# Two attention layers with 32 heads of 16, blended by a gate: products with V in wider pieces, and a new order of steps over four rounds

## The chip, the cores and the metric

The kernel runs on one core of one Trainium2 chip. The metric is the device time of one execution in microseconds. "Before" is the kernel as it stood, "after" the one with the change.

## The reference

Two attention layers A and B read the same `x` (2048 tokens of 512) with weights of their own, and a gate blends their outputs:

```python
def layer(x, wqkv, wo):                      # B, S, D = 1, 2048, 512;  H = 32, Dh = 16
    qkv = (x @ wqkv).reshape(B, S, 3, H, Dh).transpose(2, 0, 3, 1, 4)
    q, k, v = qkv[0], qkv[1], qkv[2]
    scores = jnp.einsum("bhqd,bhkd->bhqk", q, k) * (Dh ** -0.5)
    p = _softmax(scores, axis=-1)
    o = jnp.einsum("bhqk,bhkd->bhqd", p, v)
    return o.transpose(0, 2, 1, 3).reshape(B, S, D) @ wo

g = _sigmoid((x * gate_w).sum(-1, keepdims=True))
return g * layer(x, A_wqkv, A_wo) + (1 - g) * layer(x, B_wqkv, B_wo)
```

All inputs and the output are float32.

## The kernel before

Two layers of 32 heads make 64 heads, and every head has 16 tiles of 128 tokens, so there are 64 * 16 = 1024 **rounds** (`ROUNDS`). A prologue (up to about 288 us) projects q, k and v, keeps q and k as sums of two float16 parts in DRAM (`qd`, `kd`) and v in DRAM (`vd`). After that the loop `while r < ROUNDS` does the attention, and the output projection of finished layers is fed in between.

A head's q and k lie stacked on partitions in `q_st[h % 3]` and `k_st[h % 3]`, once in the lower and once in the upper 64 partitions (`load_stacks` fills both by 12 DMAs of SP's queue). One **bank** is a PSUM tile of 128 x 512, filled by four matmuls that each use a tile of 64 rows x 32 columns of TensorE's array. There are two sets of four such tiles: `tiles_of(0)` and `tiles_of(1)`. Products with V always use set 0, and `next_tiles` gives a bank of scores to the set that has had less to do, counted in `load`.

The work of the loop is of five kinds, and a letter stands for each in the string `FULL`:

- `e`: one bank of scores of keys against queries (`score`, L220), on which ScalarE then computes the exponential into the tile `p` in SBUF (L222). The bank is one of four named `ps_st`.
- `m`: one bank of scores of queries against keys of a head that comes later (`max_plain`), of which VectorE takes the maximum of each row (L158). The bank is one of three named `ps_m`.
- `D`: a bank of `ps_st` whose positive part ScalarE writes to SBUF as `rise` (`max_rise`, L165); `A`: a bank of `ps_m` to which VectorE adds that `rise` and takes the maximum of the sum (`max_pair`, L170). Each such pair replaces two banks of maxima.
- a digit: so many blocks of 128 queries of the product of `p` with V (`attend_next`, `attend`, L720), added up over 16 tiles of keys in the one bank `acc`. A digit is cut where a tile `p` ends after four blocks, and what is left is one **piece**: one instruction group of four matmuls over 128, 256, 384 or 512 columns. After each 16 tiles `p`, VectorE or ScalarE copies `acc` to SBUF (`attended`, L743), and SP's queue writes it to DRAM.
- `Q` and `R`: one step of the queue `row_ops` (small work of VectorE and ScalarE), if there is one. At the end of a head's maxima, the queue gets `max_split`, three empty steps and `max_rows`: the latter transposes the row maxima on VectorE (L187), writes them to DRAM (L190) and reads them back as two further rows of `q_st` (L192), which the head's `e` banks need.

`FULL` holds one **pass** over four rounds: 16 `e`, 12 `m`, 2 `D`, 2 `A`, and 32 blocks of products with V. It is run for r = 2, 6, ..., 998, so 250 times; the last 22 rounds use the string `LATE` instead. The string is the order in which the instructions are issued: each engine works through its own instructions in this order and waits at semaphores for the others. Products with V lag behind the exponentials by four tiles `p` (eight `e`), of the eight buffers that there are.

```python
            elif step.isdigit():
                for a in projects:
                    project_out(*a)
                    load[:] = [0, 0]
                projects.clear()
                for _ in range(attend_next(int(step))):
```

Steps of the output projection come due at given rounds (`due`). Their loads, sums and splits run on SP's queue and GpSimd; `project_out` itself (L587, 12 or 9 matmuls over the whole array, then VectorE) goes ahead of the first digit, four tiles of 128 tokens at a time.

Of the kernel before, what the change touches and what calls it, by code (L numbers as in the profile page):

```python
# [54 lines left out]
def gated_mha(ctx: ExitStack, tc: tile.TileContext, xT, x, wqkv_a, wo_a, wqkv_b, wo_b, gate_w, out):  # L55
# [703 lines left out]
                ended += u % 2  # L759
        return ended  # L760

    FULL = "QDQemQ2e1m1e2em1Qe1m2eQ1Dm1e2AQ1em1e3mem1e1Q2e1m1e1m1e1m1e1RQ2mReA"
    LATE = "e2" * 8
    projects, row_ops = [], []

# [15 lines left out]
    while r < ROUNDS:  # L781
        m = r + NT + LEAD
        if m >= ROUNDS and not ring:
            ring.append(6)
        order = FULL if m < ROUNDS else LATE
        n = order.count("e") // 4
# [70 lines left out]
```

## Time and profile before

| | |
|---|---|
| median of 3 runs | 2845.35 us (2840.07 to 2850.31) |
| profiled execution | 2855.93 us, span of the trace 2854.1 us |
| mean granted clock of TensorE | 0.994 |
| TensorE matmul busy (PE) | 2589.7 us, 91% |
| TensorE weight load busy (PEld) | 1856.0 us, 65% |
| VectorE busy (DVE) | 2405.9 us, 84% |
| ScalarE busy (ACT) | 2414.3 us, 85% |
| GpSimd busy (POOL) | 325.3 us, 11% |
| first and last `D` of a pass on ScalarE | 287.7 and 2773.8 us |

The busy time of matmuls is a union of overlapping intervals whose ends are modelled, since matmuls are pipelined and two sets of tiles work side by side; it is no measure of how full the array is. In the trace a float32 matmul and its weight load each stand as two instructions, so a piece of four matmuls makes 8 matmuls and 8 weight loads, and a bank of scores (float16) makes 4 and 4. A row of the timeline or of the groups names line, engine, operation, what is written and read, and the shape; "x" is the count; what stands behind a bar or in brackets is the idle time of the engine just before, and what ended it. "issue" there is idle time of the engine that no wait for another engine explains.

### The profile page before, as it was taken

The page shows a single profiled execution, that of the slowest core. Times are in us where ns is not written, and L with a number is a line of the kernel's source. Part 1 is how long each engine was busy: PE and PEld are TensorE (multiplying, and loading weights), DVE is VectorE, ACT ScalarE, POOL GpSimd, SP SyncE. Part 2 cuts the span into 40 slices and gives each one's busy share as a digit, 9 for nine tenths or more (in the row PEclk, how much of TensorE's full clock was granted, in tenths as well). Part 3 has the DMA queues.
Part 4 walks back from the last instruction along what each step waited for, and adds up shares of the span by engine and source line. Part 5 has one row for each costly group of instructions (what it writes and reads, how often), then busy time and mean ns, then how long its engine had stood idle before and what let it go on. Part 6 is the DMA issues. An engine that isn't in the chain of part 4 may idle for free.

```text
span 2854.1 us, 181748 instructions
## 1 busy us (share of the span) xinstructions
PE 2589.7 (91%) x83094; PEld 1856.0 (65%) x83094; DVE 2405.9 (84%) x4538; ACT 2414.3 (85%) x4794; POOL 325.3 (11%) x583
## 2 busy tenths in 40 slices
PE   9999898999999988898888898999989988888898
PEld 7787666666666666666666666666666666666664
DVE  4434898999999999999888777899999999988784
ACT  4222999999999999999999776899999999988696
POOL 2010211110000000000100432000000001022303
PEclk9999999999999999999999999999999999999999
DMA  5352222211111111111112232111111121123112
GB/s 201 113 164 97 64 58 69 60 51 41 54 39 47 46 56 45 47 46 52 52 44 73 87 106 65 40 48 45 56 37 44 46 60 56 45 66 103 61 32 106
DMA packets 110938, 187.09 MB, mean 66 GB/s; under 512 B 27944, under 2 KB 46744, under 8 KB 110168
## 3 DMA queue, kind: packets, MB, share of 16 engines
q1 hardware_dynamic: 106456, 164.97, 18.1%
q8 instruction: 650, 10.65, 1.6%
q0 software_dynamic: 2560, 8.91, 1.1%
q10 hardware_dynamic: 1152, 1.57, 0.2%
q14 instruction: 120, 0.98, 0.1%
HBM read 109.33 MB, written 66.05 MB: 61 GB/s over the span
## 4 chain that ended last, share of the span: by engine, by line
PE 68%; DVE 14%; issue 9%; ACT 5%; DMA 3%; SPq 1%; POOL 0%; ACTq 0%; DVEq 0%; POOLq 0%
PE acc L720 30%; PE ps_st L220 13%; PE ps_m L152 12%; DVE mxp L158 10%; PE ps_st L300 6%; ACT p L222 4%; PE ps_st L353 3%; PE ps_m L587 3%; DVE rise L170 2%; PE ps_st L152 2%; DMA o_part<-od 1%; DVE ev L743 1%; ACT ev L743 1%; ACT rise L165 1%; DMA q_st<-qd 0%
## 5 line engine op out<-in xcount | busy, mean ns | idle before, releaser
L222 ACT ACTIVATE p<-ps_st 128x512 f32<-128x512 f32 x4051 | 2146.5, 675 | 208.7 <-PE ps_m L152 104.5
L720 PE MATMUL acc<-p,vg 64*17 64x128 f32 (+2 forms) x48672 | 2066.3, 308 | 157.7 <-issue 139.9
L158 DVE TENSOR_REDUCE mxp<-ps_m 128x1 f32<-128x512 f32 x3048 | 1920.8, 682 | 208.0 <-PE ps_m L152 130.6
L220 PE MATMUL ps_st<-q_st,k_st 50*32 50x512 f16 x16220 | 1640.6, 381 | 46.8 <-issue 36.0
L720 PEld LDWEIGHTS acc<-p,vg 64*17 64x17 f32 x48672 | 1325.1, 93 | 385.0 <-issue 238.0
L152 PE MATMUL ps_m<-k_st,q_st 48*32 48x512 f16 x14192 | 1486.4, 381 | 42.7 <-issue 30.2
L152 PEld LDWEIGHTS <-q_st 48*32 48x32 f16 x16384 | 584.1, 90 | 317.0 <-issue 212.3
L220 PEld LDWEIGHTS <-k_st 50*32 50x32 f16 x16384 | 582.7, 90 | 205.9 <-issue 129.5
L170 DVE CUSTOM_DVE_ANT_0 rise<-ps_m,rise 128x512 f32<-128x512 f32 x500 | 341.6, 683 | 29.9 <-PE ps_m L152 14.3
L165 ACT ACTIVATE rise<-ps_st 128x512 f32<-128x512 f32 x500 | 337.0, 674 | 5.6 <-PE ps_st L152 4.8
L152 PE MATMUL ps_st<-x_st,q_st 48*32 48x512 f16 x2000 | 210.6, 380 | 4.0 <-issue 2.7
L180 POOL TENSOR_SCALAR mrow<-mrow 128x16 f32<-128x16 f32 x64 | 16.5, 257 | 1724.9 <-DVE mrow L179 1724.9
L320 ACT ACTIVATE parts<-ps_st 128x512 f16<-128x512 f32 x64 | 38.0, 596 | 112.2 <-PE ps_st L300 105.5
L321 DVE SCALAR_TENSOR_TENSOR parts<-ps_st,parts 128x512 f16<-128x512 f32 x64 | 44.0, 691 | 96.2 <-ACT parts L320 90.1
L356 ACT COPY v_st<-ps_st 128x512 f32<-128x512 f32 x32 | 18.8, 588 | 82.1 <-PE ps_st L353 80.2
L587 PE MATMUL ps_m<-wo,ot 128*128 128x512 f32 x348 | 84.5, 398 | 2.1 <-DVE mxp L158 1.9
L587 PEld LDWEIGHTS ps_m<-wo,ot 128*128 128x128 f32 x348 | 65.6, 191 | 19.7 <-issue 3.5
L559 POOL TENSOR_TENSOR o_num<-o_num,o_part 128x512 f32<-128x512 f32 x32 | 40.8, 1276 | 234.2 <-DMA o_part<-od 234.2
L300 PE MATMUL ps_st<-xh,whi 128*128 128x512 f32 x224 | 59.9, 389 | 0.0
L300 PE MATMUL ps_st<-xh,wlo 128*128 128x512 f32 x224 | 59.9, 389 | 0.0
L300 PE MATMUL ps_st<-xl,whi 128*128 128x512 f32 x224 | 59.9, 389 | 0.0
L300 PEld LDWEIGHTS ps_st<-xh,wlo 128*128 128x128 f32 x224 | 42.0, 188 | 8.7
(122 smaller groups left out, 994.7 us busy)
## 6 DMA issues: line engine op xcount, KB each, us to landing
od<-ev SPq DMA_DIRECT2D x126, 256.0 KB
k_st<-kd SPq DMA_DIRECT2D x128, 128.0 KB
q_st<-qd SPq DMA_DIRECT2D x128, 128.0 KB
vd<-v_st SPq DMA_DIRECT2D x32, 272.0 KB
vg<-vd POOLq DMA_DIRECT2D x32, 272.0 KB, 3.5
qd<-parts SPq DMA_DIRECT2D x32, 256.0 KB
kd<-parts SPq DMA_DIRECT2D x32, 256.0 KB
k_st<-kd SPq DMA_DIRECT2D x128, 64.0 KB
```

The costliest lines, as they stand in the source:

```text
L152: pe.matmul(ps[j:j + 32], q[b:b + SC, t * P + j:t * P + j + 32], k[b:b + SC], start=True, stop=True, tile_position=(b, j))
L158: dve.tensor_reduce(o[:, c:c + 1], ps, op=ALU.max, axis=AX.X)
L165: act.activation(rises[m], ps, AF.Relu)
L170: dve.tensor_tensor_reduce(out=rise, in0=ps, in1=rise, scale=1.0, scalar=LOWEST, op0=ALU.add, op1=ALU.max, accum_out=o[:, 0:1])
L220: pe.matmul(ps[j:j + 32], k[b:b + SC + 2, kk * P + j:kk * P + j + 32], q[b:b + SC + 2, cc * 512:(cc + 1) * 512], start=True, stop=True, ti ...
L222: act.activation(pt[u][:, c * 512:(c + 1) * 512], ps, AF.Exp, scale=SCALE / UNIT ** 2)
L300: pe.matmul(ps, w[a][:, k], (xh, xl)[b][cc][:, k], start=n == 0, stop=n == 3 * KC - 1)
L321: dve.scalar_tensor_tensor(pt[1][:, sl], ps, UNIT, pt[0][:, sl], op0=ALU.mult, op1=ALU.subtract)
L353: pe.matmul(ps, a[:, k, o:o + P], b[:, k], start=n == 0, stop=n == 3 * KC - 1)
L587: pe.matmul(ps, ot[a][:, slot, tt * P:(tt + 1) * P], wt[b][:, g], start=first and i == 0, stop=last and i == 2)
L720: pe.matmul(acc[d:d + 17, qa * P:qb * P], v[b:b + 64, 2 * (w % n) + c if h == NH - 1 else w % n, j], pt[u][b:b + 64, c * 512 + qa * P:c * ...
L743: (dve.tensor_copy if w < NT or h == NH - 2 else act.copy)(ev, acc)
```

## The change

One line differs: the string `FULL`. It holds the same 16 `e`, 12 `m`, 2 `D`, 2 `A`, 8 `Q`, 2 `R` and 32 blocks in another order, and the blocks stand in 12 digits (2 2 4 3 1 4 4 3 1 2 2 4) where there were 24 (mostly 1 and 2, one 3). No digit of either string is cut further.

```diff
-    FULL = "QDQemQ2e1m1e2em1Qe1m2eQ1Dm1e2AQ1em1e3mem1e1Q2e1m1e1m1e1m1e1RQ2mReA"
+    FULL = "QQD2mee2me4mQemQe3Dme1m4eme4Qme3eARRQe1m2eme2me4QeQmeA"
```

TensorE, in the first pass, before: a piece of one block between a bank of `m` and a bank of `e` (each bank is four such pairs of weight load and matmul, of which the one next to the piece is shown; `x4` are the four tiles of the array).

```order
L152 LDWEIGHTS q_st_165
L152 MATMUL ps_m<-k_st_166,q_st_165 32x512
L720 MATMUL acc<-raw,vg 17x128 x4
L220 LDWEIGHTS k_st_161
L220 MATMUL ps_st<-q_st_160,k_st_161 32x512
```

And after, in a later pass, at the first `4` of the string:

```order
L220 LDWEIGHTS k_st_161
L220 MATMUL ps_st<-q_st_160,k_st_161 32x512
L720 MATMUL acc<-p,vg 17x512 x4
L220 LDWEIGHTS k_st_161
L220 MATMUL ps_st<-q_st_160,k_st_161 32x512
```

One piece of 512 columns stands where four blocks were issued in several pieces with banks between them. On TensorE the program has 72354 such rows before and 69354 after; the 3000 that are gone are 12 pieces of each of 250 passes.

VectorE, around the end of a head's maxima, before: the copy of `acc`, the last maxima of the head (L158, L170), `max_split` (L179) and `max_rows` (L187).

```order
L158 TENSOR_REDUCE mxp<-ps_m 128x1 x6
L743 COPY ev<-acc 128x512
L158 TENSOR_REDUCE mxp<-ps_m 128x1
L170 ISA rise,mxp<-ps_m,rise 128x512
L170 ISA mxp 128x1
L179 TENSOR_REDUCE mrow<-mxp 128x16
L158 TENSOR_REDUCE mxp<-ps_m 128x1 x4
L187 STREAM_TRANSPOSE mt<-mparts 128x32
L158 TENSOR_REDUCE mxp<-ps_m 128x1
```

And after:

```order
L158 TENSOR_REDUCE mxp<-ps_m 128x1 x3
L743 COPY ev<-acc 128x512
L158 TENSOR_REDUCE mxp<-ps_m 128x1
L170 ISA rise,mxp<-ps_m,rise 128x512
L170 ISA mxp 128x1
L179 TENSOR_REDUCE mrow<-mxp 128x16
L158 TENSOR_REDUCE mxp<-ps_m 128x1 x7
L187 STREAM_TRANSPOSE mt<-mparts 128x32
L158 TENSOR_REDUCE mxp<-ps_m 128x1
```

The copy of `acc` stands ahead of the same one `m` and the `A`; the transposition of the row maxima has moved from behind four `m` to behind seven. In the string it stood behind the sixth `e` of a pass, and now stands behind the eighth. The instructions of GpSimd and of SP's queue stand in the same order as before.

## The prediction

> **What bounds the kernel now.** I read the page first, for the shares of the engines and the queues.
>
> ```profile
> span 2854.1 us, 181748 instructions
> PE 2589.7 (91%) x83094; PEld 1856.0 (65%) x83094; DVE 2405.9 (84%) x4538; ACT 2414.3 (85%) x4794; POOL 325.3 (11%) x583
> ...
> q8 instruction: 650, 10.65, 1.6%
> ...
> PE 68%; DVE 14%; issue 9%; ACT 5%; DMA 3%; SPq 1%; POOL 0%; ACTq 0%; DVEq 0%; POOLq 0%
> ```
>
> Three engines are nearly full, and 9% of the chain that ended last is "issue": TensorE waits, and no other engine is the reason. Queue q8 carries instructions: 10.65 MB in 650 packets is 16384 bytes each. TensorE has 83094 + 83094 = 166188 recorded instructions; over 650 packets that is 255.7 each. So I take q8 for TensorE's own instructions, 256 a packet, 64 bytes each.
>
> Next, the waits in a stretch of the loop without output projection (600 to 1400 us): who waited for what, us in total, times, longest.
>
> ```profile
> PEld acc L720 <- issue: 79.4, 116, 1.5
> PEld L152 <- issue: 77.3, 224, 1.6
> ...
> PE acc L720 <- issue: 42.6, 87, 1.2
> PEld L220 <- issue: 34.5, 84, 1.2
> DVE mxp L158 <- PE ps_m L152: 33.5, 84, 1.1
> ACT p L222 <- PE ps_st L220: 22.2, 56, 1.1
> ...
> PEld acc L720 <- ACT ev L743: 6.9, 14, 0.9
> PEld acc L720 <- DVE ev L743: 6.7, 14, 0.8
> ```
>
> VectorE and ScalarE wait for TensorE, and TensorE for "issue". Where do those waits end? I took them from the timeline and asked for the time from one end to the next (length; busy and count by engine):
>
> ```profile
> 903.27 0.27 PE L720 MATMUL acc<-p,vg 64*17 64x128 f32 x1 [0.58 <-issue]
> ...
> 884.18:888.20 4.02, 3.04 (x128) 2.40 (x128) 3.82 (x8) 3.64 (x8) 0.00 (x0) 1.00 0.06 12
> 888.20:891.94 3.74, 3.29 (x128) 2.38 (x128) 3.25 (x7) 3.01 (x7) 0.00 (x0) 1.00 0.02 4
> 903.27:906.73 3.46, 3.04 (x128) 2.57 (x128) 2.91 (x7) 3.46 (x8) 0.00 (x0) 1.00 0.28 97
> 906.73:910.75 4.02, 3.31 (x128) 2.38 (x128) 3.79 (x8) 3.81 (x9) 0.91 (x2) 1.00 0.09 23
> ```
>
> From one stall to the next TensorE runs 128 matmuls and 128 weight loads, exactly 256, in all four rows, whatever these are. That is one packet of q8: TensorE has run dry of instructions, and a refill takes 3.46 to 4.02 us. The stretch as a whole says the same.
>
> ```profile
> 600.00:1400.00 800.00, 721.01 (x26921) 516.48 (x26908) 746.86 (x1428) 770.75 (x1538) 36.76 (x117) 1.00 0.17 48
> ...
> q8 instruction: 210, 3.44, 1.9%
> ```
>
> 210 refills in 800 us are 3.81 us each, inside the range that the stalls give: the stream of instructions runs at its own limit nearly all the time. The Trainium skill (Runtime: NRT & Kernel Launch, section "Instruction fetch mechanics") has refills in blocks of 16 KiB, 256 instructions, with which these rows agree; it also says that fetch is hidden, since dispatch is slower than refill, and gives TensorE room for 2048 instructions. The stalls after every 256 speak against that part here.
>
> **The passes.** Two `D` stand in each pass, so the count of L165 gives passes per stretch (length; busy and count on ScalarE):
>
> ```profile
> 290.00:600.00 310.00, 43.43 (x64) 1.00 0.21 62
> 600.00:1400.00 800.00, 111.86 (x169) 1.00 0.17 48
> 1400.00:1570.00 170.00, 21.34 (x34) 1.00 0.18 53
> 1570.00:1800.00 230.00, 24.10 (x36) 0.97 0.25 80
> 1800.00:2540.00 740.00, 106.50 (x156) 1.00 0.17 49
> 2540.00:2775.00 235.00, 29.12 (x41) 0.96 0.22 67
> ```
>
> The four ordinary stretches hold 423 `D`, 211.5 passes, in 2020 us: 9.55 us a pass. The two with output projection hold 38.5 passes in 465 us: 12.08 us. A pass of before has 32 banks of scores with 8 instructions each and 24 pieces with 16 (4 float32 matmuls and 4 weight loads, each in two): 256 + 384 = 640, or 2.5 refills; at 3.81 us that is 9.53 us. The 9.55 are explained.
>
> **What the change removes.** 12 pieces of 16 instructions in each of 250 passes: 192 of 640 go. 448 are left, 1.75 refills, at 3.81 us 6.7 us a pass. The stream is then no longer the limit, and what is late next has to be found: the two engines that empty the banks, or the array.
>
> Their pace without a wait, from rows in which they work back to back (start, length, count):
>
> ```profile
> 927.37 3.04 ACT L222 ACTIVATE p<-ps_st 128x512 f32<-128x512 f32 x6
> 930.24 0.67 ACT L165 ACTIVATE rise<-ps_st 128x512 f32<-128x512 f32 x1
> ...
> 931.69 4.27 DVE L158 TENSOR_REDUCE mxp<-ps_m 128x1 f32<-128x512 f32 x7
> 935.88 0.68 DVE L170 CUSTOM_DVE_ANT_0 rise<-ps_m,rise 128x512 f32<-128x512 f32 x1
> 936.48 0.08 DVE L170 DVE_READ_ACCUMULATOR2_ANT mxp<- 128x1 f32 x1
> 936.48 0.68 DVE L158 TENSOR_REDUCE mxp<-ps_m 128x1 f32<-128x512 f32 x1
> ```
>
> ScalarE: (930.24 - 927.37) / 6 = 0.478 us a bank. A pass has 16 `e` and 2 `D`, and a copy of `acc` every fourth pass, taken at the same pace: 18.25 x 0.478 = 8.72 us. VectorE: (935.88 - 931.69) / 7 = 0.599 us an `m`, 0.60 an `A`: 14 x 0.60 = 8.39, a copy of `acc` every fourth pass (0.15), and a head's small steps, some 0.1: 8.65 us. So a pass can't go below 8.72 us, and both engines are within 0.1 us of that.
>
> The array: a piece costs what its columns cost. Instances of L720 by shape:
>
> ```profile
> L720 PE MATMUL acc<-p,vg 64*17 64x128 f32 x11440 | 473.9, 270 | 35.8 <-issue 35.5
> L720 PE MATMUL acc<-p,vg 64*17 64x256 f32 x4036 | 347.3, 378 | 11.0 <-issue 7.1 <-ACT ev L743 1.6 <-DVE ev L743 0.4
> L720 PE MATMUL acc<-p,vg 64*17 64x384 f32 x676 | 76.0, 483 | 0.0
> ...
> 903.53 0.54 PE L720 MATMUL acc<-p,vg 64*17 64x384 f32 x4
> 903.72 0.39 PE L220 MATMUL ps_st<-q_st,k_st 50*32 50x512 f16 x4
> 903.86 0.54 PE L720 MATMUL acc<-p,vg 64*17 64x384 f32 x4
> 903.94 0.39 PE L152 MATMUL ps_m<-k_st,q_st 48*32 48x512 f16 x4
> ```
>
> Each further 128 columns add 105 to 108 ns, so a block costs 2 x 0.107 = 0.21 us in whatever piece (a piece is issued in two halves). 32 blocks are 6.8 us of set 0, in both orders. The banks of scores run beside them: one starts at 903.72 between the two halves of the 384-column piece, the next at 903.94, 0.22 us later. 32 x 0.22 = 7.0 us on set 1. Both are under 8.72, so the array covers what goes and does not replace it.
>
> **What is moved.** Wider pieces bunch the array's work, and the 3 + 4 banks between TensorE and the other two must cover the bunches. The longest is `m4eme4Qm`: a 512-column piece should hold set 0 for 4 x 0.21 = 0.86 us, in which set 1 can fill four banks; nothing starves if scores overtake as above. No row shows 512 columns; bounds: 0 if they behave as the 384 do, and at the far end what the third rival prices. I take 0.05 us a pass for this.
>
> The piece reads a `p` whose last `e` lies at least five `e` back (six before). There are four `ps_st` banks, so the fifth `e` could be issued only after that bank had been emptied: the wait costs nothing. The copy of `acc` is followed by five banks until the next piece where there were six; the waits for it are 6.9 + 6.7 us in 84 passes now, 0.16 a pass, and I allow 0.08 more.
>
> `max_rows` moves from behind the sixth `e` to behind the eighth, and SP's rows show its slack:
>
> ```profile
> 883.86 0.58 SPq L190 DMA_DIRECT2D md<-mt  x1
> 885.83 0.55 SPq L192 DMA_DIRECT2D q_st<-md  x2
> 893.77 0.56 SPq L114 DMA_DIRECT2D k_st<-kd  x1
> ```
>
> The write takes 1.97 us until its data may be read back; if the read takes as long after its issue at 886.1, it has landed at 888.4. The reload of the old head's stack goes out at 893.77, when its last scores are done and those of the new head begin: 5.4 us of slack. Two `e` of 0.6 us and a pass that is 0.7 us shorter take 1.9 of it. 3.5 are left: nothing. The loads and stores of SP and GpSimd keep their order and rounds, and come 7% sooner with slack of rounds.
>
> **The sum.** A pass of 8.72 + 0.05 + 0.08 = 8.85 us in the ordinary stretches: 211.5 x (9.55 - 8.85) = 148 us. In the two stretches with projection, `project_out` keeps all three engines waiting in bursts that don't change; I take half the gain for their passes: 38.5 x 0.35 = 13 us. Together 161 us. The profiled execution took 2855.93 us and would take 2695; the median of the runs is 10.6 us under it, 2845.35 - 161 = 2684. I say 2685.
>
> **Rivals.** First, the bunches cost more than I allow. Only 7 banks cover them, and VectorE and ScalarE must both be kept 98% busy from one queue of instructions; before, ScalarE reached 770.75 of 800 us, or 96%, in finer steps. At 95% of ScalarE's floor a pass takes 9.18: 250 x 0.37 = 92, or 2753 us; down to no gain at 9.5.
>
> Second, the "issue" waits aren't the limit, or don't shrink with the count: TensorE would lose as much per pass with 448 instructions, in fewer and longer waits, and the time stays at 2845 +- 8.5 (0.3%, about what a measurement can tell from no change). The 256 between stalls speak against it. By the Trainium skill's statement that fetch is hidden (same page and section) the gain would be 0, the time 2845, and the 9% of "issue" something else.
>
> Third, slower: a 512-column piece doesn't let scores pass. If the four of a pass ran alone, TensorE would need 4 x 0.86 + 7.0 = 10.4 us, and more with the two pieces of 384. That is 0.9 us over before, 250 x 0.9 = 225: 3070 us. It becomes a loss where the two sets lose over 9.55 - 7.0 = 2.55 us a pass of their side by side. The 384-column row speaks against it.
>
> **Numbers.** Forecast 0.67 (2640 to 2730), bunches 0.20 (2730 to 2835), no change 0.06, slower 0.07. The low end of the range is a pass at its floor everywhere: 250 x 0.83 = 207, 2638, so 2640. The upper end takes in most of the first rival: 2765. Faster 0.87, same 0.06, slower 0.07.
>
> **What would show it.** q8 with 462 packets ((166188 - 48000) / 256); no stall of "issue" each 256 instructions, and its share of the chain at 2% or less; ScalarE at 97% or more between 600 and 1300 us; L165 counted 2 per 8.85 us; 512-column matmuls at about 590 ns (483 + 107), with scores starting inside them. I am wrong if TensorE's waits for `ps_m` or `ps_st` leave ScalarE under 95%, if refills take much longer than 4 us, or if the piece behind the copy of `acc` waits over 0.5 us a pass.

## The result, and the profile after

| | before | after |
|---|---|---|
| median of 4 runs | 2843.68 us (2840.07 to 2850.31) | 2689.16 us (2687.98 to 2691.21) |
| span of the profiled execution | 2854.1 us | 2686.2 us |
| a pass in the ordinary stretches | 9.55 us | 8.99 us |
| a pass in the stretches with output projection | 12.08 us | 10.99 us |

The ratio is 0.9455, with a 95% interval from 0.9436 to 0.9474. The forecast was 2685 us.

The page of after, the lines that answer to those shown of before:

```profile
span 2686.2 us, 133748 instructions
PE 2591.5 (96%) x59094; PEld 1441.2 (54%) x59094; DVE 2388.0 (89%) x4538; ACT 2374.2 (88%) x4794; POOL 325.1 (12%) x583
...
q8 instruction: 462, 7.57, 1.2%
...
PE 53%; ACT 24%; DVE 14%; issue 7%; DMA 2%; SPq 0%; POOL 0%; ACTq 0%; DVEq 0%; POOLq 0%
```

TensorE has 48000 instructions fewer and q8 has 462 packets, both as forecast. ScalarE's part of the chain that ended last has risen from 5% to 24%. The waits of after between 600 and 1300 us, the longest first, without those of GpSimd:

```profile
PEld L152 <- issue: 108.9, 405, 0.5
PEld L220 <- issue: 105.4, 519, 0.7
...
PEld acc L720 <- ACT ev L743: 17.2, 20, 0.9
...
PEld acc L720 <- DVE ev L743: 13.9, 19, 0.9
...
DVE mxp L158 <- PE ps_st L220: 4.7, 16, 0.3
```

"PE acc L720 <- issue", 42.6 us before in a slightly longer stretch, is no longer in the list, nor are ScalarE's and VectorE's waits of 22 and 33 us for TensorE. What is left under "issue" are weight loads that stand idle 0.2 to 0.3 us at a time while matmuls run.

The same stretch by engine (length; busy and count):

```profile
600.00:1300.00 700.00, 676.01 (x17478) 350.60 (x17462) 685.59 (x1322) 698.83 (x1426) 26.02 (x93) 1.00 0.17 50
```

And the count of `D` on ScalarE by stretch of after:

```profile
290.00:1480.00 1190.00, 242.49 (x265) 1.00 0.18 54
1480.00:1698.00 218.00, 33.92 (x38) 0.99 0.29 93
1698.00:2400.00 702.00, 141.44 (x156) 1.00 0.17 52
2400.00:2605.00 205.00, 34.55 (x39) 1.00 0.21 69
```

ScalarE is busy 698.83 of 700 us: it is the limit now, at 700 / 1426 = 0.491 us an operation. VectorE follows with 685.59. 421 `D` in 1892 us are 8.99 us a pass, and 77 in 423 us are 10.99.

### The profile page after: what moved, and what is told of

Read it like the earlier page. It is cut to its first block, busy times and chain, and to the rows that moved or that the text cites. A ratio compares the mean times of both kernels' runs of the same rounds, so it can differ in the third digit from the quotient of the medians.

```text
span 2686.2 us, 133748 instructions
## 1 busy us (share of the span) xinstructions
PE 2591.5 (96%) x59094; PEld 1441.2 (54%) x59094; DVE 2388.0 (89%) x4538; ACT 2374.2 (88%) x4794; POOL 325.1 (12%) x583
## 4 chain that ended last, share of the span: by engine, by line
PE 53%; ACT 24%; DVE 14%; issue 7%; DMA 2%; SPq 0%; POOL 0%; ACTq 0%; DVEq 0%; POOLq 0%
ACT p L222 20%; PE acc L720 18%; PE ps_m L152 11%; PE ps_st L220 10%; DVE mxp L158 10%; PE ps_st L300 6%; PE ps_st L353 3%; DVE rise L170 3%; PE ps_m L587 3%; ACT ev L743 2%; ACT rise L165 2%; DMA o_part<-od 1%; PE ps_st L152 1%; DVE mrow L179 0%; DVE ev L743 0%
## 5 line engine op out<-in xcount | busy, mean ns | idle before, releaser
L222 ACT ACTIVATE p<-ps_st 128x512 f32<-128x512 f32 x4051 | 2200.8, 861 | 87.7 <-PE ps_st L220 83.7
L720 PE MATMUL acc<-p,vg 64*17 64x256 f32 (+3 forms) x24720 | 2005.0, 448 | 64.1 <-ACT ev L743 33.8
L158 DVE TENSOR_REDUCE mxp<-ps_m 128x1 f32<-128x512 f32 x3048 | 1895.1, 681 | 76.4 <-PE ps_st L152 43.5
L220 PE MATMUL ps_st<-q_st,k_st 50*32 50x512 f16 x16220 | 1554.9, 381 | 6.3 <-issue 0.3
L152 PE MATMUL ps_m<-k_st,q_st 48*32 48x512 f16 x14192 | 1409.0, 379 | 14.6 <-DVE mxp L158 3.2
L220 PEld LDWEIGHTS <-k_st 50*32 50x32 f16 x16384 | 649.5, 90 | 501.9 <-issue 342.3
L152 PEld LDWEIGHTS <-q_st 48*32 48x32 f16 x16384 | 596.0, 90 | 476.1 <-issue 353.3
L720 PEld LDWEIGHTS acc<-p,vg 64*17 64x17 f32 x24720 | 544.5, 92 | 179.4 <-issue 56.8
L165 ACT ACTIVATE rise<-ps_st 128x512 f32<-128x512 f32 x500 | 454.7, 909 | 0.0
L170 DVE CUSTOM_DVE_ANT_0 rise<-ps_m,rise 128x512 f32<-128x512 f32 x500 | 341.6, 683 | 18.1 <-PE ps_st L220 2.0
L743 ACT COPY ev<-acc 128x512 f32<-128x512 f32 x62 | 53.7, 866 | 0.0
```

The costliest lines, as they stand in the source:

```text
L152: pe.matmul(ps[j:j + 32], q[b:b + SC, t * P + j:t * P + j + 32], k[b:b + SC], start=True, stop=True, tile_position=(b, j))
L158: dve.tensor_reduce(o[:, c:c + 1], ps, op=ALU.max, axis=AX.X)
L165: act.activation(rises[m], ps, AF.Relu)
L170: dve.tensor_tensor_reduce(out=rise, in0=ps, in1=rise, scale=1.0, scalar=LOWEST, op0=ALU.add, op1=ALU.max, accum_out=o[:, 0:1])
L220: pe.matmul(ps[j:j + 32], k[b:b + SC + 2, kk * P + j:kk * P + j + 32], q[b:b + SC + 2, cc * 512:(cc + 1) * 512], start=True, stop=True, ti ...
L222: act.activation(pt[u][:, c * 512:(c + 1) * 512], ps, AF.Exp, scale=SCALE / UNIT ** 2)
```

## The experiments

Each kernel was timed beside the kernel before. "Ordinary" and "projection" are the lengths of a pass in the two kinds of stretches, taken between the same `A` steps in each trace (9.60 and 12.06 us for before, 8.99 and 10.99 for after, on this count). Before took 2843.68 us beside after, 2849.92 beside e1 to e4, 2851.92 beside e5 to e8 and 2831.26 beside e9 to e12. Differences to after are those of the times; by the ratios they would be some 6 to 9 us smaller for e6 and e8 and 9 to 14 us larger for e9 to e12. The lengths of the passes, which need no second kernel, agree with the times to some 3 us.

| run | instructions a pass | time, us | ordinary | projection |
|---|---|---|---|---|
| before | 640 | 2843.68 | 9.60 | 12.06 |
| after | 448 | 2689.16 | 8.99 | 10.99 |
| e1, new order, 24 pieces | 640 | 2854.16 | 9.56 | 11.85 |
| e2, new order, 18 pieces | 544 | 2705.33 | 8.99 | 11.38 |
| e3, new order, 32 pieces | 768 | 3281.96 | 11.39 | 13.52 |
| e4, old order, 12 pieces | 448 | 2709.70 | 8.97 | 11.72 |
| e5, scores in halves | 704 | 3070.67 | 10.49 | 12.79 |
| e6, after, more on ScalarE | 448 | 2829.69 | 9.57 | 11.43 |
| e7, before, more on ScalarE | 640 | 2889.67 | 9.72 | 12.28 |
| e8, new order, 8 pieces | 384 | 2721.54 | 9.11 | 11.16 |
| e9, after, rows earlier | 448 | 2715.02 | 8.99 | 11.71 |
| e10, after, rows later | 448 | 2687.75 | 8.98 | 10.93 |
| e11, old order, 12 pieces, rows later | 448 | 2685.44 | 8.96 | 11.13 |
| e12, after, split on VectorE | 448 | 2744.00 | 9.18 | 11.46 |

The first four separate the number of pieces from the order of the steps.

```diff
 after: FULL = "QQD2mee2me4mQemQe3Dme1m4eme4Qme3eARRQe1m2eme2me4QeQmeA"
 e1:    FULL = "QQD11mee11me22mQemQe21Dme1m112eme22Qme21eARRQe1m11eme11me112QeQmeA"
 e2:    FULL = "QQD11mee2me22mQemQe3Dme1m22eme22Qme3eARRQe1m11eme2me22QeQmeA"
 e3:    FULL = "QQD11mee11me1111mQemQe111Dme1m1111eme1111Qme111eARRQe1m11eme11me1111QeQmeA"
 e4:    FULL = "QDQemQ2em2eem4Qem2eQDm2eAQ4eme4meme2Qe2me4mem2eRQ2mReA"
```

> The new order of steps, with its 12 pieces cut at their places into 24 (a 2 as 1 1, a 4 as 2 2 or 1 1 2, two of the 3 as 2 1), so 640 instructions of TensorE a pass as before the change. Theory (refills of 256 instructions, 3.81 us each): 2.5 refills, 9.5 us a pass, some 2830 us, and stalls of issue every 256 instructions again. Rival (the order of the steps made the gain, not the count): 2690 us.

Measured: 2854.16 us, ratio to before 1.0021 (1.0001 to 1.0041). With 24 pieces the new order gains nothing in total. TensorE's waits "PE acc L720 <- issue", gone in after, are back with 22.9 us between 600 and 1300 us.

> The new order with 18 pieces: 544 instructions a pass. Theory: 2.125 refills are 8.1 us, still under the 8.97 us that ScalarE needs, so no change from after: 2690 us (within 10). Rival (each piece has a cost of its own, 154 us for 12 more): half of it, 2766 us.

Measured: 2705.33 us, ratio 0.9516 (0.9493 to 0.9540). The ordinary pass is the same as in after, 8.99 us, with 50% more pieces: a piece has no cost of its own while the refills keep up. The total is 16 us over after, where at most 10 were expected, and the 16 come from the stretches with projection. Refills are 5.5 us apart there on average, but work comes in bursts. In the first of these stretches TensorE stops seven times for more than 1 us, together 13 us, with "issue" as the only reason, and in the second once for 2.6 us. In after its matmuls have one such stop in both, 1.4 us. The time from the end of one stop to the end of a later one, four rows of six (matmuls are the first count, weight loads the second):

```profile
1492.43:1498.37 5.94, 4.45 (x129) 2.62 (x128) 4.33 (x7) 4.51 (x9) 4.06 (x5) 1.00 0.47 177
1498.37:1530.35 31.98, 28.41 (x897) 17.30 (x897) 28.61 (x54) 29.54 (x60) 12.80 (x16) 1.00 0.31 92
1538.14:1578.58 40.44, 38.62 (x895) 25.56 (x896) 30.20 (x55) 28.25 (x57) 14.44 (x17) 1.00 0.23 72
1584.53:1631.10 46.57, 42.71 (x1024) 27.98 (x1023) 34.59 (x64) 32.23 (x65) 19.31 (x22) 1.00 0.32 98
```

But for a record or two these are 256 instructions, 7 x 256, 7 x 256 and 8 x 256: here too the stops come at the ends of refills. So a mean count under the limit isn't enough where the work is bunched.

> The new order with all 32 blocks as pieces of their own: 768 instructions a pass. Theory: 3.0 refills, 11.4 us a pass, 250 x 2.46 us over after: 3300 us. Rival (each piece has a cost of its own): 20 pieces more at 154/12 us each, 2946 us. Rival (order): 2690 us.

Measured: 3281.96 us, ratio 1.1546 (1.1484 to 1.1608), 18 us from the theory and 336 from the nearer rival. Between 600 and 1300 us of its trace, each of 150 stops of TensorE of over 0.4 us ends a multiple of 256 instructions after the end of the one before, give or take 4 records; in before it is each of 74, in after 2 of 35.

> The old order of e, m, D, A, Q and R, with the blocks merged into 12 pieces at places where pieces stood before (2 2 4 2 2 4 4 2 2 4 2 2): 448 instructions a pass. Theory: most of the gain, 2690 to 2715 us, the rest being the order's share in feeding ScalarE. Rival (order made the gain): 2800 us or more.

Measured: 2709.70 us, ratio 0.9530 (0.9500 to 0.9560): 21 us over after, all of it in the stretches with projection. In the ordinary ones the old order is as good.

The packets of q8 in the same 700 us show the limit directly (packets, MB, share), here in the order before, e1, e3, e5, and then after and e2:

```profile
q8 instruction: 185, 3.03, 1.9%
```

```profile
q8 instruction: 183, 3.00, 1.8%
```

```profile
q8 instruction: 185, 3.03, 1.9%
```

```profile
q8 instruction: 184, 3.01, 1.8%
```

```profile
q8 instruction: 136, 2.23, 1.3%
```

```profile
q8 instruction: 165, 2.70, 1.7%
```

Four kernels with 640, 640, 768 and 704 instructions a pass take between 183 and 185 refills in 700 us, one each 3.8 us, whatever a pass does. The two others ask for fewer and get what they ask for.

e5 raises the count without touching the products with V:

```diff
         for b, j in next_tiles():
-            pe.matmul(ps[j:j + 32], ..., k[b:b + SC], start=True, stop=True, tile_position=(b, j))
+            for f in (0, 256):
+                pe.matmul(ps[j:j + 32, f:f + 256], ..., k[b:b + SC, f:f + 256], start=True, stop=True, ...)
```

> After, with each matmul of the loop's score banks issued as two of 256 columns (each with its weight load): 512 + 192 = 704 instructions a pass, the same work for the array, and the 12 pieces with V untouched. Theory (count of instructions, whichever they are): 2.75 refills, 10.5 us a pass, 250 x 1.5 us over after: 3065 us. Rival (something particular to the pieces with V was the cost): under 2750 us.

Measured: 3070.67 us, ratio 1.0767 (1.0705 to 1.0829), and 10.49 us a pass where 2.75 x 3.81 is 10.48. It is the count, whichever instructions make it.

e6 and e7 add the same work of ScalarE to both kernels:

```diff
         act.activation(rises[m], ps, AF.Relu)
+        if m % 4 == 0:
+            act.activation(rises[m], ps, AF.Relu)
```

> After, with one of the two D of a pass computed twice on ScalarE (into the same tile): one activation of 128x512 more a pass. Theory (ScalarE is the limit of after): 250 x 0.49 = 122 us more, 2811 us. Rival (another engine or the banks are the limit): under 2730 us.

> Before, with the same one activation more a pass. Theory (refills are the limit of before, ScalarE has 9.55 - 8.94 = 0.6 us a pass to spare): 0 to 40 us more, 2845 to 2885 us. Rival (ScalarE was the limit before as well): 122 us more, 2967 us.

Measured: 2829.69 us for after with it (140.5 more; ratio to before 0.9926, 0.9900 to 0.9952), and 2889.67 for before with it, ratio 1.0130 (1.0090 to 1.0170), some 38 us more. So ScalarE is the limit of after and had most of this to spare before. The 140.5 are over the 122 expected; the timeline of e6 shows why one activation was dearer there:

```profile
908.56 0.82 ACT L165 ACTIVATE rise<-ps_st 128x512 f32<-128x512 f32 x1
909.41 0.60 ACT L167 ACTIVATE rise<-ps_st 128x512 f32<-128x512 f32 x1
909.90 2.55 ACT L224 ACTIVATE p<-ps_st 128x512 f32<-128x512 f32 x5
```

The second one writes the same tile and starts only when the first has ended, 0.85 us after its start, where others follow each other at 0.48.

e8 goes further with wide pieces:

```diff
+    FULL = "QQDmee4me4mQemQe4Dmem4eme4Qme4eARRQememe4me4QeQmeA"
```

> The new order with 8 pieces of 512 columns: 384 instructions a pass, 1.5 refills. Theory: ScalarE's pace stays the limit, 2685 to 2700 us. Rival (each piece has a cost of its own): 4 x 154/12 = 51 us less, 2638 us.

Measured: 2721.54 us, ratio 0.9537 (0.9500 to 0.9574), 32 us slower than after: both missed. The ordinary pass is 0.12 us longer and ScalarE's busy time falls to 694.13 of 700 us (its row below). Coarser steps do cost, as the first rival of the prediction had it, but only with all 32 blocks in pieces of 512 columns. Through which wait they cost it is not shown.

```profile
600.00:1300.00 700.00, 689.78 (x14768) 339.79 (x14755) 679.51 (x1307) 694.13 (x1405) 24.75 (x92) 1.00 0.16 47
```

What makes the 21 us between e4 and after? The traces differ at `max_rows`: in the stretches with projection VectorE's transposition waits for GpSimd, which does the sums and splits of the output projection, and with it wait the maxima behind it, their banks, and TensorE. Three runs move it alone:

```diff
-            row_ops += [(max_split, m // NT), (None,), (None,), (None,), (max_rows, m // NT)]
+            row_ops += [(max_split, m // NT)] + [(None,)] * 2 + [(max_rows, m // NT)]   # e9; 4 in e10 and e11
```

> After, with max_rows one step of the queue earlier (two empty steps ahead of it): the transposition stands behind four m again, as before the change. Theory (its later place is what the new order gains over the old one with 12 pieces, 20 us, because GpSimd is late with its input while it works for the output projection): some 2705 to 2710 us, all of it in the stretches with projection. Rival (the place of the other steps makes it): 2685 to 2695 us.

> After, with max_rows one step later (four empty steps): behind eight m and an A. Theory of its place: VectorE's waits for GpSimd, 12.6 us in after, shrink, 2678 to 2689 us. Rival (the rows then come too late for the head's first e, since 3.5 us of slack were left by the estimate and 1 us goes): over 2700 us.

> The old order with 12 pieces, with max_rows one step later: behind five m and an A. Theory of its place: VectorE's waits for GpSimd (21.9 us) halve, and with them most of the 20 us over after goes: 2688 to 2700 us. Rival (the place of the other steps): 2705 to 2715 us.

Measured: e9 2715.02 us, ratio 0.9593 (0.9576 to 0.9610); e10 2687.75, 0.9496 (0.9480 to 0.9513); e11 2685.44, 0.9489 (0.9472 to 0.9506). One place earlier costs the new order 26 us, one place later saves the old order 24, and the ordinary pass doesn't move. VectorE's idle time ahead of the transposition, first e9, then after, then e10 (us, times):

```profile
  POOL mparts L182: 23.1, 9
```

```profile
  POOL mparts L182: 12.6, 6
```

```profile
  POOL mparts L182: 1.2, 2
```

In before these waits came to 5.4 us, at the place of e9: they grow when the passes get faster. In e11 they are 12.8 us, where e4 has 21.9. What they do to TensorE shows in the waits of the first stretch with projection, first of e9, then of after:

```profile
DVE mt L187 <- POOL mparts L182: 17.5, 4, 7.6
PE ps_m L152 <- DVE mxp L158: 15.2, 4, 6.9
```

```profile
DVE mt L187 <- POOL mparts L182: 11.1, 4, 4.0
...
PE ps_m L152 <- DVE mxp L158: 1.8, 1, 1.8
```

In e9 the wait reaches TensorE, which finds no free `ps_m` bank for 15.2 us; in after all but 1.8 us of VectorE's 11.1 stays off TensorE. That also fits e10: from after to e10 11 us of VectorE's waits go and the time does not follow. TensorE's granted clock differs with it. It is the third figure from the end of these rows (they count the transpositions of the stretch), for e9, e4 and e11:

```profile
1480.00:1700.00 220.00, 1.05 (x5) 0.95 0.28 90
```

```profile
1480.00:1700.00 220.00, 1.04 (x5) 0.96 0.28 88
```

```profile
1480.00:1700.00 220.00, 1.06 (x5) 0.99 0.28 91
```

After has 0.99 there as well. How much of the 26 and 24 us is the lower clock and how much the waits themselves was not separated. The rows were not late for the head's scores in e10 either. By their times e10 and e11 are not told apart from after (1 and 4 us under it), and by their ratios they are 12 and 10 us over it; the passes of e10 are as long as those of after to 0.06 us.

e12 takes GpSimd out of that step:

```diff
-        pool.tensor_scalar(m, m, 1.0 / TOP, None, op0=ALU.mult)
-        pool.tensor_copy(mp[:, 0], m)
-        pool.tensor_tensor(mp[:, 1], m, mp[:, 0], op=ALU.subtract)
+        dve.tensor_scalar(m, m, 1.0 / TOP, None, op0=ALU.mult)
+        dve.tensor_copy(mp[:, 0], m)
+        dve.tensor_tensor(mp[:, 1], m, mp[:, 0], op=ALU.subtract)
```

> After, with the three small steps between the row maxima and their transposition on VectorE in place of GpSimd, so that VectorE waits for nobody there. Theory: the waits for GpSimd (12.6 us) go, VectorE has 0.1 us more a pass and stays under ScalarE's 8.97: 2675 to 2687 us. Rival (VectorE, 98% busy, is as much the limit as ScalarE): 2695 to 2715 us.

Measured: 2744.00 us, ratio 0.9680 (0.9650 to 0.9711), 55 us slower than after, more than the rival's 26. Its timeline of VectorE:

```profile
927.96 0.22 DVE L179 TENSOR_REDUCE mrow<-mxp 128x16 f32<-128x64 f32 x1
928.22 0.17 DVE L180 TENSOR_SCALAR mrow<-mrow 128x16 f32<-128x16 f32 x1
928.43 0.17 DVE L181 CAST mparts<-mrow 128x16 f16<-128x16 f32 x1
928.63 0.17 DVE L182 TENSOR_TENSOR mparts<-mrow,mparts 128x16 f16<-128x16 f32 x1
928.73 4.27 DVE L158 TENSOR_REDUCE mxp<-ps_m 128x1 f32<-128x512 f32 x7
```

Each step waits for the one before, 0.77 us from the first to the next maximum, where after has 0.14. The list of its waits between 600 and 1300 us has what follows:

```profile
PE ps_m L152 <- DVE mxp L158: 16.5, 22, 1.2
```

TensorE waits for `ps_m` (0.6 us in the same list of after) and holds up the exponentials behind it: ScalarE's waits for `ps_st` are 8.9 us in this list and 0.2 us in that of after. The 0.63 us more a head cost 0.19 us a pass, 0.76 a head, in the ordinary stretches: VectorE has nothing to give at this place, and after stands at the pace of both engines. What the waits for GpSimd cost e12 does not settle, since it also adds work.

## Why the prediction was right, and where its terms were off

**The limit before, right.** Refills of TensorE's instructions at 3.81 us per 256: e1, e3 and e5 follow the count to within 30 us of their forecasts, and e2 shows the knee on its other side. The Trainium skill (Runtime: NRT & Kernel Launch, "Instruction fetch mechanics") calls fetch hidden. Here 183 to 185 refills in 700 us, in four kernels, say that it can be the limit, and the measurement decides.

**The term of the ordinary stretches, 148 us forecast, 8.99 against 8.85 us a pass: 211 x (9.60 - 8.99) = 129 us.** The step that was off is ScalarE's pace, taken as 0.478 us from one short row. Starts do follow at that distance, but not for long. The group of the page of after, and its timeline of ScalarE:

```profile
L222 ACT ACTIVATE p<-ps_st 128x512 f32<-128x512 f32 x4051 | 2200.8, 861 | 87.7 <-PE ps_st L220 83.7
```

```profile
909.19 6.00 ACT L222 ACTIVATE p<-ps_st 128x512 f32<-128x512 f32 x11
914.61 1.06 ACT L165 ACTIVATE rise<-ps_st 128x512 f32<-128x512 f32 x1
```

These eleven take 914.61 - 909.19 = 5.42 us, 0.493 each, and the mean of one has grown from 675 to 861 ns: in a long row without a gap each lasts longer, the ends fall 0.49 apart, and from time to time a start waits. The ends show the pace: the median from one end to the next is 0.490 us in before, after and e6 alike, while starts run ahead of it after a pause. So with ScalarE busy 698.83 of 700 us, its 0.491 us an operation is its pace and not a wait. 18.25 x 0.491 = 8.96 us gives the measured pass but for 0.03, as it must with the same count of operations; e6 is the test of it. So the 0.13 us that I allowed for bunches and for the copy of `acc` were not lost as such; e4 with the old order has 8.97. The waits for the copy did grow, from 0.16 to 0.40 us a pass (17.2 + 13.9 us in 78 passes) where I allowed 0.24, but ScalarE had banks to work on meanwhile.

**The array, right.** The group of the widest shape in after, and in its timeline a piece of 512 columns with the banks of scores that start inside it:

```profile
L720 PE MATMUL acc<-p,vg 64*17 64x512 f32 x2496 | 312.7, 592 | 0.0
```

```profile
926.77 0.61 PE L720 MATMUL acc<-p,vg 64*17 64x512 f32 x4
926.92 0.40 PE L152 MATMUL ps_m<-k_st,q_st 48*32 48x512 f16 x4
927.13 0.40 PE L220 MATMUL ps_st<-q_st,k_st 50*32 50x512 f16 x4
927.20 0.61 PE L720 MATMUL acc<-p,vg 64*17 64x512 f32 x4
```

592 ns where 590 were forecast, two banks between its halves: the rival that was slower had no ground.

**The term of the projection stretches, 13 us forecast, 38.5 x (12.06 - 10.99) = 41 us measured.** The step that failed is `max_rows`: I priced its move at nothing, looking only at the slack behind it, which held. 2.8 us are left, where 3.5 were forecast: the write goes out at 956.14, the read at 958.12, the reload at 963.41. (The landing at 888.4 in the prediction counts from the end of the read's issue, 886.4; from 886.1, as it says, it would be 888.1, with 0.3 us more slack.)

```profile
956.14 0.58 SPq L190 DMA_DIRECT2D md<-mt  x1
958.12 0.55 SPq L192 DMA_DIRECT2D q_st<-md  x2
963.41 0.59 SPq L114 DMA_DIRECT2D k_st<-kd  x1
```

I didn't ask who was late ahead of it. By e9 the move is worth 26 us, all in these stretches; the rest, 12.06 - 11.71 = 0.35 us in 38.5 passes, 13 us, is what I had allowed for the count. That the bursts don't change was not so either: in the first stretch VectorE waits 22.1 us for the banks of `project_out` where it waited 33.0, and TensorE's granted clock in the two stretches is 0.99 and 1.00, where it was 0.97 and 0.96. The two misses, 19 us too much and 28 too little, leave the gain of the traces 9 us larger than forecast, 129 + 41 = 170 us. The gain of the medians is 154.5, mostly since the profiled execution of before was 12 us longer than its median. So the forecast is 4 us from the result partly by luck: the sum was better than its terms.

**Signs.** 462 packets, ScalarE over 97% and, in the ordinary stretches, no stall of matmuls on issue came true; two `D` per 8.85 us did not, it is 8.99. The share of issue on the chain, forecast at 2% or less, is 7%. In the ordinary stretches the chain now passes through other idle time of TensorE that it gives that name, in pieces of 0.5 us at most between 600 and 700 us, and the sign was a poor one.

## What to carry to other kernels

Count TensorE's instructions, not only its columns: where a stretch takes one refill of 256 each 3.8 us, matmuls of half the size cost time although the array isn't full, and once the count is under the next limit, in the bursts as well as in the mean, fewer instructions bring nothing more. Find the pace of an engine from a long full stretch, not from a short row. When a step is moved, look at who is late ahead of it as well as at who waits behind it.

## What the runs showed of the hardware that I had not expected

A float32 matmul of the program counts four times against the refills (two matmuls and two weight loads), a float16 one twice. Activations of 128x512 can start 0.478 us apart for a while, but hold only 0.491 over 700 us. Dependent steps of 128x16 on VectorE start 0.2 us apart.
